# Two of four x tiles transposed by the DMA instead of PE at the start of the key stage, with their plain load moved to ScalarE's queue

## The chip, the cores and the metric

The kernel runs on one core of one Trainium2 chip. The metric is the device time of one execution in microseconds.

Engines: PE (TensorE, matmul), DVE (VectorE), ACT (ScalarE), POOL (GpSimd) and SP (SyncE). SP and ACT also issue DMA transfers. I call the transfers issued by one of them its ring.

## The reference, cut to what matters

```python
def _A_ref(x, wqkv, wo):          # linear attention, 32 heads of 16
    q, k, v = split(x @ wqkv)
    phi = lambda t: where(t > 0, t + 1, exp(t)) + 1e-6
    pq, pk = phi(q), phi(k)
    kv = einsum("bhsd,bhse->bhde", pk, v); z = pk.sum over s
    o = (pq @ kv) / (pq . z + 1e-6)
    return o @ wo
def _B_ref(x, w1, b1, w2, b2):    # token mixer: layernorm, w1 over tokens, gelu, w2
    ...
g = sigmoid((x * gate_w).sum(-1))
return g * _A_ref(...) + (1 - g) * _B_ref(...)
```

x is 2048 x 512 in bf16, in 16 tiles of 128 rows. The key stage computes `x @ Wk`. That needs every x tile transposed (`xT`) as the stationary operand, and Wk in four blocks of 128 rows, called Wk rows 0 to 3 here.

## The kernel before

The parts that the change touches (cuts marked):

```python
    def load_xT(t0, n):           # DMA transpose straight from HBM, always on SP
        nc.sync.dma_start(out=xT[:, :, t0*P:(t0+n)*P], in_=X[t0*P:(t0+n)*P, :], transpose=True)

    load_x(nc.sync, 0, 1)
    load_x(nc.scalar, 1, 1)
    load_wk(nc.sync, 0)
    load_x(nc.scalar, 2, 1)
    load_x(nc.sync, 3, 1)
    for k, q in ((1, nc.scalar), (2, nc.sync), (3, nc.scalar)):
        load_wk(q, k)
    load_xT(4, 2)
    load_xT(6, 2)
    load_x(nc.sync, 4, 4)
    ...                           # tiles 8-15, Wq, w1, Wv, Wo, all on SP
    nc.scalar.activation(out=act_warm[:], in_=ones_f[:], func=ACT.Exp)   # brings the table load
    warm_up(6)                    # six dummy matmuls on constants
    ...
    HEADS = 4
    transpose_tile(0, False)      # four PE transposes into PSUM, evacuated by DVE
    transpose_tile(1, True)       # ... evacuated by ACT
    transpose_tile(2, False)
    for k in range(2):
        for t in range(HEADS - 1):
            k_part(t, (k,))       # key matmul of tile t with Wk row k
    transpose_tile(HEADS - 1, True)
    for t in range(HEADS):
        k_part(t, range(2 if t < HEADS - 1 else 0, ND))
        k_phi(t)
    LAG = 4
    for t in range(HEADS, NT):
        k_part(t, range(ND)); k_phi(t)
        g_tile(t - LAG)           # gacc matmuls: x^T times phi(k)
        ...
```

The order of instructions on each engine is as written. In this kernel's trace the loads from SP and ACT share eight completion semaphores in turn, so the ninth and later ones wait until the earlier load of the same semaphore has landed.

## Time and profile before

| | before |
|---|---|
| median, us | 165.53 (165.50 to 165.75, 4 runs) |
| span of the profile, us | 163.4 |
| PE busy | 158.7 us, 97% |
| first gacc matmul | 9.93 us |
| last matmul of the kernel | 160.37 us |

From the page (first line: the span; then busy time; then 40 slices of 4.1 us, in tenths of the slice, and the DMA's GB/s):

```profile
span 163.4 us, 2099 instructions
PE 158.7 (97%) x787; PEld 73.3 (45%) x801; DVE 88.3 (54%) x202; ACT 58.7 (36%) x90; POOL 18.3 (11%) x37
PE   7999999999999999999999999999999999999993
PEclk9999999999999999999999999999999999999999
GB/s 152 235 237 213 280 308 328 349 349 348 326 130 0 0 0 247 202 4 0 286 299 101 181 320 279 323 121 88 36 32 32 32 32 32 45 52 35 32 32 32
```

PE is full from the second slice to the last. So only the start can change the time, and a shift there reaches the end. The chain of waits of the first 12 us (start, length, what) says how the start goes:

```profile
0.81 2.98 DMA xs<-in_A_x_dram
3.84 1.05 PE pt L195 x8
4.91 0.61 ACT xT L199
5.56 1.29 PE kacc L108 x5
6.85 0.22 PE pt L195 x4
7.08 3.02 PE kacc L108 x14
10.10 0.86 PE gacc L108 x4
```

The x tiles land, PE transposes tiles 0 and 1 (`pt`), and ACT copies tile 1. From 5.56 us there is only PE. ACT was ready in time, as its timeline shows (start, length, instruction; in brackets the idle time before it and what ended it):

```profile
2.67 1.28 ACT L189 ACT_TABLE_LOAD   x1 [2.67 <-issue]
3.96 0.20 ACT L189 ACTIVATE act_warm<-ones_f 128x1 f32<-128x1 f32 x1
4.91 0.60 ACT L199 ACTIVATE xT<-pt 128x512 bf16<-128x512 bf16 x1 [0.74 <-PE pt L195]
```

### The profile page before, as it was taken

The numbers are of one execution on the slowest core, as the hardware profiler recorded it, in microseconds if no ns is written. First come the engines' busy times: TensorE is split into PE (matmuls) and PEld (weight loads), VectorE is DVE, ScalarE is ACT, GpSimd is POOL, SyncE is SP. The second block draws the span as 40 slices with busy tenths as digits, with TensorE's granted clock in tenths as the row PEclk, the third lists the DMA queues.
The fourth block names the chain that finished last, engine by engine and source line by source line (L and its number), as shares of the span: only waits on it lengthen the run. The fifth ranks groups of instructions, "written<-read, shape, count | busy, mean of one in ns | idle before, by whom it ended". The sixth has DMA issues, their size and how long they took to land.

```text
span 163.4 us, 2099 instructions
## 1 busy us (share of the span) xinstructions
PE 158.7 (97%) x787; PEld 73.3 (45%) x801; DVE 88.3 (54%) x202; ACT 58.7 (36%) x90; POOL 18.3 (11%) x37
## 2 busy tenths in 40 slices
PE   7999999999999999999999999999999999999993
PEld 2544444444444444444444444444444444444452
DVE  1599999957999999029995301156221111111112
ACT  3463386648676483111222213111112222111110
POOL 5000711200100000001055500050000000000000
PEclk9999999999999999999999999999999999999999
DMA  5999999999950007600893599932100000111001
GB/s 152 235 237 213 280 308 328 349 349 348 326 130 0 0 0 247 202 4 0 286 299 101 181 320 279 323 121 88 36 32 32 32 32 32 45 52 35 32 32 32
DMA packets 30057, 25.05 MB, mean 153 GB/s; under 512 B 7968, under 2 KB 29472, under 8 KB 30048
## 3 DMA queue, kind: packets, MB, share of 16 engines
q1 hardware_dynamic: 28032, 22.02, 45.5%
q0 software_dynamic: 1440, 2.38, 5.5%
q10 hardware_dynamic: 576, 0.52, 1.1%
q8 instruction: 6, 0.10, 0.3%
q14 instruction: 3, 0.02, 0.0%
HBM read 21.11 MB, written 2.23 MB: 143 GB/s over the span
## 4 chain that ended last, share of the span: by engine, by line
PE 95%; DMA 2%; issue 1%; ACT 0%; DVE 0%
PE uacc L108 30%; PE yps L108 29%; PE aps L108 9%; PE gacc L108 8%; PE qacc L108 8%; PE kacc L108 8%; DMA xs<-in_A_x_dram 2%; PE pt L195 1%; PE denps L108 1%; PE wps L108 1%; PE kvps L108 0%; ACT xT L199 0%; DVE ot L481 0%; PE zps L108 0%; PE pt L324 0%
## 5 line engine op out<-in xcount | busy, mean ns | idle before, releaser
L108 PE MATMUL uacc<-hs,w1c 128*128 128x512 bf16 x219 | 51.8, 379 | 0.4
L108 PE MATMUL yps<-uT,w2c 128*128 128x512 bf16 (+2 forms) x234 | 50.6, 366 | 0.2
L481 DVE SCALAR_TENSOR_TENSOR ot<-yps,c,a_sc 128x512 bf16<-128x512 f32 (+2 forms) x17 | 12.2, 720 | 46.0 <-PE yps L108 42.7
L108 PEld LDWEIGHTS <-w2c 128*128 128x128 bf16 x238 | 22.8, 98 | 25.9
L108 PEld LDWEIGHTS <-w1c 128*128 128x128 bf16 x224 | 21.7, 98 | 26.3 <-issue 0.4
L468 ACT ACTIVATE a_sc<-aps,c,gg 128x512 f32<-128x512 f32 x16 | 12.4, 778 | 46.7 <-PE aps L108 43.0
L318 ACT ACTIVATE uT<-uacc,bcol 128x512 bf16<-128x512 f32 x14 | 9.3, 687 | 28.3 <-PE uacc L108 28.3
L108 PE MATMUL aps<-W2sb,pqT 128*128 128x512 bf16 x63 | 16.4, 379 | 0.1
L108 PE MATMUL qacc<-xT,wq_sb 128*128 128x512 bf16 x63 | 16.2, 379 | 0.0
L108 PE MATMUL kacc<-wk_sb,xT 128*128 128x512 bf16 x63 | 16.0, 380 | 0.1
L108 PE MATMUL gacc<-pk,xs 128*128 128x512 bf16 x62 | 15.5, 379 | 0.1
L245 ACT ACTIVATE hs<-xs,nmr,rstd 128x512 bf16<-128x512 bf16 x16 | 12.8, 805 | 1.9 <-DVE nmr L239 1.9
L205 ACT ACTIVATE e<-qacc 128x512 bf16<-128x512 f32 x16 | 9.6, 597 | 9.2 <-PE qacc L108 8.3
L419 POOL DMA_DIRECT2D rex<-rd_dram x16 | 9.4, 602 | 23.0 <-DVE pqT L421 17.5
L205 ACT ACTIVATE e<-kacc 128x512 bf16<-128x512 f32 x16 | 9.3, 595 | 6.9 <-PE kacc L108 5.6
L209 DVE SCALAR_TENSOR_TENSOR pk<-kacc,e 128x512 bf16<-128x512 f32 x16 | 11.1, 692 | 0.6
L209 DVE SCALAR_TENSOR_TENSOR pqT<-qacc,e 128x512 bf16<-128x512 f32 x16 | 11.1, 692 | 0.6
L229 DVE BATCH_NORM_STATS2 stats<-xs 128x6 f32<-128x512 bf16 x16 | 10.9, 682 | 0.0
L206 DVE TENSOR_SCALAR e<-e 128x512 bf16<-128x512 bf16 x32 | 9.0, 282 | 3.1 <-ACT e L205 3.1
L406 DVE CUSTOM_DVE_ANT_0 junk<-xs,gw_b 128x512 bf16<-128x512 bf16 x16 | 9.9, 684 | 0.0
L270 DVE TENSOR_TENSOR zacc<-zacc,pk 128x512 f32<-128x512 f32 x14 | 9.6, 686 | 0.2
L108 PEld LDWEIGHTS <-pqT 128*128 128x128 bf16 x64 | 6.3, 98 | 7.6
(65 smaller groups left out, 69.6 us busy)
## 6 DMA issues: line engine op xcount, KB each, us to landing
w2c<-in_B_w_dram SPq DMA_DIRECT2D x8, 896.0 KB, 6.6
w1c<-in_B_w_dram SPq DMA_DIRECT2D x2, 2048.0 KB, 15.7
w1c<-in_B_w_dram SPq DMA_DIRECT2D x3, 1024.0 KB, 12.9
rex<-rd_dram POOLq DMA_DIRECT2D x16, 128.0 KB, 3.2
out_dram<-ot SPq DMA_DIRECT2D x15, 128.0 KB, 1.7
xs<-in_A_x_dram SPq DMA_DIRECT2D x3, 512.0 KB, 5.1
wq_sb<-in_A_wqkv_dram SPq DMA_DIRECT2D x1, 512.0 KB, 7.1
wv_sb<-in_A_wqkv_dram SPq DMA_DIRECT2D x1, 512.0 KB, 11.4
```

The lines of the kernel that those rows point to most:

```text
L108: nc.tensor.matmul(o, lhsT=lhsT, rhs=rhs, start=start, stop=stop, **kw)
L205: nc.scalar.activation(out=e[:], in_=acc[:], func=ACT.Exp)
L206: nc.vector.tensor_scalar(out=e[:], in0=e[:], scalar1=1.0, scalar2=PHI_EPS, op0=ALU.min, op1=ALU.add)
L209: nc.vector.scalar_tensor_tensor(out=dst, in0=acc[:], scalar=0.0, in1=e[:], op0=ALU.max, op1=ALU.add)
L229: nc.vector.bn_stats(out=stats[:], in_=xs[:, t, :])
L245: nc.scalar.activation(out=hs[:, t, :], in_=xs[:, t, :], func=ACT.Identity, scale=rstd[:, t : t + 1], bias=nmr[:, t : t + 1],)
L270: nc.vector.tensor_tensor(out=zacc[:], in0=first, in1=pk[:, t, :], op=ALU.add)
L318: nc.scalar.activation(out=uT[:, j, :], in_=acc[:], func=ACT.Gelu_apprx_tanh, bias=bcol[:, j : j + 1])
L406: nc.vector.tensor_tensor_reduce(out=junk[:], in0=xs[:, t, :], in1=gw_b[:], scale=1.0, scalar=0.0, op0=ALU.mult, op1=ALU.add, accum_out=gp ...
L419: nc.gpsimd.dma_start(out=rex[:], in_=src.unsqueeze(1).to_broadcast([8, HEAD, SC]))
L468: nc.scalar.activation(out=a_sc[:], in_=aps[:], func=ACT.Identity, scale=gg[:, t : t + 1], bias=c2[:, t : t + 1],)
L481: nc.vector.scalar_tensor_tensor(out=ot[:, :W], in0=yps[:, :W], scalar=c1[:, t : t + 1], in1=a_sc[:, cs], op0=ALU.mult, op1=ALU.add,)
```

## The change

The intent: let the DMA transpose tiles 2 and 3, so that PE opens with two tiles instead of four. Eight PE transposes and two evacuations go. Tiles 2-3 still have to be loaded plain (for `gacc` and the layernorm); that is not urgent, and goes last on ACT's ring. The four Wk rows are also dealt out anew: row 1 alone stays on SP, rows 0, 2 and 3 go on ACT. Wk row 3 is the fourth load on ACT's ring in both kernels.

```diff
     load_x(nc.sync, 0, 1)
     load_x(nc.scalar, 1, 1)
-    load_wk(nc.sync, 0)
-    load_x(nc.scalar, 2, 1)
-    load_x(nc.sync, 3, 1)
-    for k, q in ((1, nc.scalar), (2, nc.sync), (3, nc.scalar)):
-        load_wk(q, k)
+    load_wk(nc.sync, 1)
+    load_wk(nc.scalar, 0)
+    load_xT(2, 2)
+    for k in (2, 3):
+        load_wk(nc.scalar, k)
     load_xT(4, 2)
+    load_x(nc.scalar, 2, 2)
     load_xT(6, 2)
@@
-    HEADS = 4
+    HEADS = 2
     transpose_tile(0, False)
     transpose_tile(1, True)
-    transpose_tile(2, False)
     ln_step(0)
     for k in range(2):
-        for t in range(HEADS - 1):
+        for t in range(HEADS):
             k_part(t, (k,))
-    transpose_tile(HEADS - 1, True)
     ln_step(1)
     for t in range(HEADS):
-        k_part(t, range(2 if t < HEADS - 1 else 0, ND))
+        k_part(t, range(2, ND))
         k_phi(t)
@@
-        g_tile(t - LAG)
+        if t >= LAG:
+            g_tile(t - LAG)
```

## The prediction

> **What bounds the kernel now.** TensorE. The page gives PE 158.7 of 163.4 us busy; the chain that ended last is 95% PE. In the timeline, from 7.1 us on matmul follows matmul every 0.216 us, and the list of waits has no DMA wait of PE after the start. So only the start (about 10 us) can change the time, and whatever it gains or loses there is passed on whole.
>
> **The start before.** x tile 1 lands at 3.60 us, tile 0 at 3.79; PE transposes tiles 0, 1, 2 from 3.84, 0.107 us each (slow clock). VectorE copies tile 0 (4.48-4.90), first key matmul at 5.09. ScalarE copies tile 1 at 4.91-5.51, so the second key matmul starts at 5.56. From there the chain of waits is PE alone: 19 key matmuls and the four transposes of tile 3 (0.056 us each, 0.22 in all), then the first gacc matmul at 9.93. ScalarE was ready: its four loads were issued by 2.64, its table load ran 2.67-3.95, its warm-up activation to 4.16.
>
> **Removed.** Eight PE transposes and two evacuations (0.42 DVE, 0.60 ACT). Those of tile 2 lie in the shadow of the tile 0 and 1 copies; only those of tile 3, 0.22 us, are on the chain. Total with smoother order: about 0.25 us.
>
> **Added, moved.** (a) A 256-row DMA transpose as third transfer on SP, issued at about 1.75. Its like took 1.34 us to issue and 3.7-4.1 us to landing, so I estimate 5.8-6.9; tile 2 is needed at 7.1 or later. The skill (DMA: Bandwidth & Descriptors, "Issuing engines are not separate DMA queues") says all issuers share the same 16 DMA engines; some delay of the Wk loads (landing 4.4-6.5 before) is likely, little of it exposed. The next SP transfers come 0.6 us earlier; nothing waits for them.
> (b) The plain load of tiles 2-3 is the fifth issue on ACT's queue. Read instruction by instruction, it waits for the semaphore of an earlier load, that of x tile 1, which lands at 3.60. ScalarE's stream is in order, so table load, warm-up activation and the copy of tile 1 stand behind it. Issue 3.6-4.1 (0.5, as its likes), table load 1.28 -> 5.4, warm-up 0.2 -> 5.63, copy 0.60 -> 6.24. The second key matmul then starts at about 6.3 instead of 5.56: +0.74 us, on the chain, since PE's order is fixed. The skill (ScalarE: Activation LUTs, "What ACT_TABLE_LOAD costs") has 1283 ns for the load; this trace has 1283 ns twice.
>
> **Sum.** +0.74 - 0.25 = +0.5 us; first gacc at about 10.4. Everything later shifts rigidly.
>
> **Predicted: 166.05 us, 165.3 to 166.9 (8 in 10).** Faster by over 2%: 0.01; within 2%: 0.97; slower: 0.02.
>
> **What would show it.** ACT: a gap before the table load to about 4.1, table load to 5.4, copy of tile 1 at 5.6-6.2. PE: idle about 0.8 us before the second key matmul, then at least 19 key matmuls without a stop; first gacc near 10.4; no wait for xT tiles 2-3. Right in (a) if transposed tiles land before 7.5. From first gacc to the end the same length as before.
>
> **What would make it wrong.** If the ACT load does not hold the table load back, the gain of 0.25 us stands (165.3). If the DMA transpose slows Wk or lands after 7.8, PE stalls more (+0.3 to 1). PE's clock became fast at about 5.4 us; with PE idler around 4.8-6.3 it may rise later, and each key matmul in slow state costs 0.2 us more (up to +1.2).

## The result, and the profile after

The changed kernel takes 168.50 us (168.07 to 168.54, 4 runs), against 165.53 before. The ratio is 1.0171, with a 95% interval of 1.0152 to 1.0190. (Ratios are the mean of one kernel's runs over the mean of the other's of the same rounds, so not quite the ratio of the medians. Executions over 1.5% slower than the fastest of the same kernel are left out of the means.) The direction was as predicted, but the loss was 2.97 us instead of 0.5.

The same lines of the page:

```profile
span 166.5 us, 2081 instructions
PE 159.6 (96%) x779; PEld 73.0 (44%) x793; DVE 88.1 (53%) x201; ACT 58.5 (35%) x89; POOL 18.4 (11%) x37
PE   7499999999999999999999999999999999999992
PEclk9969999999999999999999999999999999999999
GB/s 140 164 202 281 267 352 314 354 348 348 332 154 0 0 0 96 345 0 4 159 351 96 162 306 284 348 123 132 31 35 31 31 31 31 31 50 48 31 31 32
```

Nearly all the difference is in the first three slices. PE is half idle in the second, its clock is down in the third, and the DMA moves 164 and 202 GB/s where it moved 235 and 237, though more is asked of it. The first gacc matmul comes at 12.88 us, 2.95 later; the last matmul of the kernel comes at 163.32, also 2.95 later. From the first gacc to the last matmul nothing has changed. (After the last matmul this trace has 3.22 us to the end of the span, and the one before 3.07.)

ACT's timeline:

```profile
3.60 0.44 ACTq L124 DMA_DIRECT2D xs<-in_A_x_dram  x1
4.08 1.28 ACT L190 ACT_TABLE_LOAD   x1 [4.08 <-DMA xs<-in_A_x_dram]
5.37 0.20 ACT L190 ACTIVATE act_warm<-ones_f 128x1 f32<-128x1 f32 x1
5.48 0.58 ACT L200 ACTIVATE xT<-pt 128x512 bf16<-128x512 bf16 x1
```

This is the hold that was predicted. The late load waits for x tile 1 (landed at 3.58), and the table load stands behind it. PE's timeline shows what was not predicted:

```profile
3.45 1.01 PE L196 MATMUL pt<-ident,xs 128*128 128x128 bf16 x8
4.58 0.39 PE L108 MATMUL kacc<-wk_sb,xT 128*128 128x512 bf16 x1
6.11 1.04 PE L108 MATMUL kacc<-wk_sb,xT 128*128 128x512 bf16 x4 [1.15 <-ACT xT L200]
8.23 4.82 PE L108 MATMUL kacc<-wk_sb,xT 128*128 128x512 bf16 x15 [1.08 <-DMA wk_sb<-in_A_wqkv_dram]
12.88 0.81 PE L108 MATMUL gacc<-pk,xs 128*128 128x512 bf16 x3
```

After the hold there is a second wait, for Wk. Then 15 matmuls take 4.82 us, where 14 took 3.02 (before, in the chain). The stretches that the clock record itself is divided into show why (per engine busy time and instructions, then the granted clock, DMA share and GB/s):

```profile
core 0: us, PE busy (x) PEld busy (x) DVE busy (x) ACT busy (x) POOL busy (x), PEclk, DMA share, GB/s
4.31:7.72 3.41, 1.58 (x7) 0.50 (x6) 1.75 (x5) 1.74 (x3) 0.00 (x0) 1.00 1.26 169
7.72:11.14 3.42, 2.91 (x7) 0.98 (x7) 1.59 (x4) 1.19 (x2) 0.00 (x0) 0.50 1.24 151
```

In the window from 4.31 to 7.72 PE was busy for only 1.58 us, and for the next 3.42 us its clock was 0.50. Seven key matmuls started about 0.42 us apart instead of 0.216.

The transfers, by tile and issue. In the kernel before, the last Wk row (asked together with row 2 of SP, which took 4.3 us; row 3 took 4.0) and the transpose of tiles 4-5:

```profile
L127 ACTq DMA_DIRECT2D wk_sb<-in_A_wqkv_dram x1: 453/453/453, 2.2 to 2.2; - x1
DMA to landing us min/median/max: 4.0/4.2/4.3
```

```profile
L130 SPq DMA_TRANSPOSE xT<-in_A_x_dram x1: 1337/1337/1337, 3.6 to 3.6; - x1
DMA to landing us min/median/max: 4.1/4.1/4.1
```

In the changed kernel, the last Wk row (issued by ACT at 2.2), then the transposes of tiles 2-3 and of tiles 4-5:

```profile
L127 ACTq DMA_DIRECT2D wk_sb<-in_A_wqkv_dram x1: 454/454/454, 2.2 to 2.2; - x1
DMA to landing us min/median/max: 6.0/6.0/6.0
```

```profile
L130 SPq DMA_TRANSPOSE xT<-in_A_x_dram x1: 1333/1333/1333, 1.7 to 1.7; - x1
DMA to landing us min/median/max: 7.1/7.1/7.1
```

```profile
L130 SPq DMA_TRANSPOSE xT<-in_A_x_dram x1: 2813/2813/2813, 3.1 to 3.1; - x1
DMA to landing us min/median/max: 8.6/8.6/8.6
```

| landed at, us | before | after |
|---|---|---|
| Wk row 3 | 6.21 | 8.19 |
| transpose of tiles 2-3 | (on PE) | 8.81 |
| transpose of tiles 4-5 | 7.67 (issued 3.62) | 11.67 (issued 3.11) |

On PE's own clock of events the 2.95 us add up. The second key matmul comes 0.55 us later (6.11 against 5.56), the wait for Wk row 3 is 1.24 (8.23 minus 6.77 minus 0.216), and the slow clock is 1.42 (seven starts in 2.93 us instead of 1.51). The removed transposes of tile 3 and small rests give back 0.26. But this is a list of what stood on PE's path one after another. It does not say what the time would be without one of them, since the transpose of tiles 4-5 landed at 11.67, only 0.35 ahead of its first use at 12.02. The experiments had to tell that.

### The profile page after: what moved, and what is told of

The parts are those of the page before. It is cut to its first block, busy times and chain, and to the rows that moved or that the text cites. A ratio compares the mean times of both kernels' runs of the same rounds, so it can differ in the third digit from the quotient of the medians.

```text
span 166.5 us, 2081 instructions
## 1 busy us (share of the span) xinstructions
PE 159.6 (96%) x779; PEld 73.0 (44%) x793; DVE 88.1 (53%) x201; ACT 58.5 (35%) x89; POOL 18.4 (11%) x37
## 4 chain that ended last, share of the span: by engine, by line
PE 93%; DMA 4%; ACTq 1%; issue 1%; DVE 0%
PE yps L108 29%; PE uacc L108 29%; PE kacc L108 8%; PE qacc L108 8%; PE aps L108 8%; PE gacc L108 8%; DMA wk_sb<-in_A_wqkv_dram 4%; PE denps L108 1%; ACTq L127 1%; PE wps L108 1%; PE kvps L108 0%; ACTq L124 0%; DVE ot L481 0%; PE zps L108 0%; PE pt L324 0%
## 5 line engine op out<-in xcount | busy, mean ns | idle before, releaser
L108 PE MATMUL kacc<-wk_sb,xT 128*128 128x512 bf16 x63 | 17.3, 406 | 2.3 <-ACT xT L200 1.1
L206 ACT ACTIVATE e<-kacc 128x512 bf16<-128x512 f32 x16 | 9.5, 595 | 11.7 <-PE kacc L108 10.4
L108 PEld LDWEIGHTS <-xT 128*128 128x128 bf16 x64 | 6.5, 103 | 11.3 <-issue 3.0
```

What stands on the lines that cost most here:

```text
L108: nc.tensor.matmul(o, lhsT=lhsT, rhs=rhs, start=start, stop=stop, **kw)
L206: nc.scalar.activation(out=e[:], in_=acc[:], func=ACT.Exp)
```

## The experiments

The theory after this reading was the three terms above. Rival A held that the ACT hold is the cause of everything. Rival B held that the slow clock is a matter of the window's phase or of the eight missing transposes, not of PE's idling. Rival C came up after the first runs: late landings go by the bytes in flight, whatever their kind. All kernels gave correct results. Each was timed beside the kernel before on the same chip, and "before" below is that of its own rounds. One execution of each run has a trace; the last column gives its first gacc and, in brackets, its time. In runs 2, 3, 7 and 9 it is the slowest execution of the run.

| run | us, median (range) | before, us | first gacc in the trace (its time) |
|---|---|---|---|
| late load after ACT's table load | 168.53 (167.39 to 169.59) | 165.63 | 11.68 (167.39) |
| Wk row 3 ahead of the transposes | 166.32 (166.19 to 167.97) | 165.63 | 11.97 (167.97) |
| both | 165.70 (165.04 to 167.06) | 165.63 | 11.73 (167.06) |
| filler matmuls | 167.79 (167.23 to 168.06) | 165.63 | 12.29 (167.97) |
| rings apart | 165.65 (165.33 to 166.12) | 165.59 | 9.53 (165.36) |
| plain loads in the transposes' place | 170.34 (167.87 to 171.49) | 165.59 | 12.87 (169.26) |
| before, 256 KB more on ACT | 166.62 (166.58 to 167.50) | 165.59 | 11.53 (167.50) |
| before, 256 KB more on SP | 166.19 (165.92 to 166.28) | 165.59 | 9.83 (166.21) |
| rings apart, loads merged | 165.40 (164.89 to 165.83) | 165.61 | 10.22 (165.83) |
| late load on SP | 166.55 (165.75 to 168.26) | 165.61 | 11.04 (166.54) |
| rings apart and ACT held | 165.76 to 167.62 (5 runs) and one of 598.72 | 165.61 | (no usable trace) |
| the same again | 165.82 and 165.99 | 165.64 and 165.70, and one of 285.17 at a clock of 0.563 | 10.45 (165.82) |

### 1. The late load after ACT's table load

```diff
-    load_x(nc.scalar, 2, 2)
     ...
     nc.scalar.activation(out=act_warm[:], in_=ones_f[:], func=ACT.Exp)
+    load_x(nc.scalar, 2, 2)
```

> The changed kernel, with the plain load of tiles 2-3 issued by ScalarE after its table load and warm-up activation instead of before. Theory (three terms: ScalarE held about 0.55 us; the last Wk row landing at 8.19 us instead of 6.2-6.5; slow PE clock for seven key matmuls after the two idle stretches): the table load goes back to about 2.7 us and the second key matmul to about 5.1 us, but PE then waits longer for the last Wk row, which still lands near 8.2; the clock still falls; time unchanged, 168.0 to 168.6. Rival A (the ScalarE hold is the cause of all of it): 165.3 to 165.6.

The median was 168.53, in two groups: 167.39 and 167.72 with a mean clock of 1.0, 169.35 and 169.59 with 0.99. PE's timeline of the traced one (167.39):

```profile
4.58 1.43 PE L108 MATMUL kacc<-wk_sb,xT 128*128 128x512 bf16 x5 [0.30 <-DVE xT L202]
8.10 2.53 PE L108 MATMUL kacc<-wk_sb,xT 128*128 128x512 bf16 x11 [2.09 <-DMA wk_sb<-in_A_wqkv_dram]
10.80 1.04 PE L108 MATMUL kacc<-wk_sb,xT 128*128 128x512 bf16 x4 [0.17 <-DMA xT<-in_A_x_dram]
```

The hold is gone (second key matmul at 4.97), and PE simply waits for Wk row 3 until 8.10. One wait of 2.09 us stands where the changed kernel had two, 1.15 and 1.08. Rival A falls: in the changed kernel the predicted hold was mostly hidden behind the DMA. The two groups lie about 1.9 us apart; the slower one has no trace, so that this is the clock alone is not shown. The traced execution had a 2 us idle stretch and no fall, so the same kernel falls into the slow clock in some executions and not in others.

### 2. Wk row 3 ahead of the first transpose, ACT still held

```diff
     load_wk(nc.scalar, 0)
+    load_wk(nc.sync, 3)
+    load_wk(nc.scalar, 2)
+    (a load of 128 x 8 elements on ACT, so that the late load still waits)
     load_xT(2, 2)
-    for k in (2, 3):
-        load_wk(nc.scalar, k)
```

> The changed kernel, with the last Wk row issued on SP ahead of the first DMA transpose; a tiny load on ACT's queue keeps ScalarE's wait as it is. Theory: the last Wk row lands by about 6.5, PE's second stall goes, and with it the slow clock; the hold of ScalarE stays (second key matmul at about 6.1). What can still cost is the transpose of tiles 2-3, which landed at 8.81 in the changed kernel and is wanted at about 7.7: 166.0 to 167.0. Rival A: unchanged, 168.5. Rival B (the last Wk row is late because it is fourth on its ring, and the slow clock is the window's phase): the stall goes, the slow clock stays, 167.2 or more.

166.32: four executions at 166.19 to 166.37, two at 167.59 and 167.97. All Wk had landed by 5.31 and the second stall went, as the theory had it. The transpose of tiles 2-3 landed at 6.13, in time. The traced execution is the slowest one. There the clock rose only at 9.62 (window 6.21 to 9.62 slow), which cost it about 1.7 us (nine starts in 3.64 us instead of 1.94). That PE's idling delayed the rise fits, but one trace does not show it.

### 3. Both edits

```diff
     load_wk(nc.scalar, 0)
-    load_xT(2, 2)
-    for k in (2, 3):
-        load_wk(nc.scalar, k)
+    load_wk(nc.sync, 3)
+    load_wk(nc.scalar, 2)
+    load_xT(2, 2)
     load_xT(4, 2)
-    load_x(nc.scalar, 2, 2)
     ...
     nc.scalar.activation(out=act_warm[:], in_=ones_f[:], func=ACT.Exp)
+    load_x(nc.scalar, 2, 2)
```

> Both edits together (without the tiny load). Theory: second key matmul at about 5.1, all Wk by 6.5, tiles 0-1 done near 7; then PE waits for the transpose of tiles 2-3 if that lands after 7. Time 165.2 if it lands by 7, 166.2 to 167 if it lands at 8 to 8.8. Rival A: 165.3 to 165.6 whatever lands when.

167.06, 165.05, 166.34 and 165.04. In the traced execution (167.06) the transpose of tiles 2-3 landed at 9.08 and the late load at 9.01, side by side on the two rings, and PE waited 2.13 us for it:

```profile
9.12 2.76 PE L108 MATMUL kacc<-wk_sb,xT 128*128 128x512 bf16 x12 [2.13 <-DMA xT<-in_A_x_dram]
```

The expectation held in its conditional form. The executions of 165.04 and 165.05 have no trace; they lie below all seven of the kernel before in these rounds (165.37 to 165.90), with the late load still on the other ring. So the two need not hurt each other in every execution. Why the same transpose lands at 6.1 in one run and at 9.1 in another was open. That led to the new theory: a transpose from one ring beside plain loads from the other makes both slow.

### 4. Filler matmuls in the second idle stretch

```diff
     ln_step(1)
+    warm_up(5)
     for t in range(HEADS):
         k_part(t, range(2, ND))
```

> The changed kernel with five more dummy matmuls on constants placed in PE's second idle stretch, between the key matmuls of Wk rows 1 and 2. Theory (the idle stretches made the clock fall): the key matmuls after 8.2 us run at 0.216 us each instead of 0.427, so more work makes it faster: 167.0 to 167.4. Rival B (the slow clock is the phase of a window, or the eight fewer PE transposes, not the idling): unchanged or slower, 168.3 to 168.6.

```profile
6.67 1.25 PE L108 MATMUL wps<-const-bfloat16-1.0 128*128 128x512 bf16 x5
7.76 0.38 PE L108 MATMUL kacc<-wk_sb,xT 128*128 128x512 bf16 x1
8.30 2.54 PE L108 MATMUL kacc<-wk_sb,xT 128*128 128x512 bf16 x11 [0.16 <-DMA wk_sb<-in_A_wqkv_dram]
11.41 1.04 PE L108 MATMUL kacc<-wk_sb,xT 128*128 128x512 bf16 x4 [0.57 <-DMA xT<-in_A_x_dram]
```

Five more matmuls made it faster: 167.79 against 168.50. All four executions had a clock of 1.0; of the changed kernel's four, three had 0.99. That is few, but the other runs agree: but for the execution of 285.17, mean clocks of 0.99 or less appear only in kernels whose traces show PE waiting about a microsecond or more (the changed kernel, runs 1, 6, 10 and 11, the last by the trace of run 12), and in none of the twelve executions of runs 5 and 9, which lack the same eight transposes (0.998 or more). So the missing transposes are not it. The window's phase may still decide in which executions the clock falls, since run 1 fell in two of four. The gain was 0.7 us, below the expected 1.1 to 1.5. With the clock fast, PE meets the next wait, the transpose of tiles 4-5 that lands at 11.37. In the changed kernel it landed at 11.67 and was first used at 12.02, so with a fast clock and the same landings only about 0.3 of the 1.42 us could have come back, and the one execution of the changed kernel with a clock of 1.0 took 168.07, 0.4 less than the others. So more than half of what the slow clock took on PE's path was in the shadow of a late transfer.

### 5. The rings kept apart

```diff
     load_wk(nc.scalar, 0)
-    load_xT(2, 2)
-    for k in (2, 3):
-        load_wk(nc.scalar, k)
+    load_wk(nc.sync, 3)
+    load_wk(nc.scalar, 2)
+    load_xT(2, 2)
     load_xT(4, 2)
-    load_x(nc.scalar, 2, 2)
     load_xT(6, 2)
+    load_x(nc.sync, 2, 2)
```

> The changed kernel with no plain load left on ACT's ring beside a transpose: ACT carries only x tile 1 and Wk rows 0 and 2, SP the rest, Wk row 3 ahead of the transposes and the plain load of tiles 2-3 behind them. New theory (from the packets of the first runs: transposes and plain loads that run at once from two rings both crawl): all Wk lands by 6.0, the transpose of tiles 2-3 between 6 and 7, that of 4-5 by 8, and this in every execution; no hold of ScalarE; time 165.0 to 165.2 with a spread below 0.5. Rival C (the landings of transposes are early or late by chance, or go by bytes): a spread of 1 to 2 us as in the run with both edits.

The landings were as expected: Wk by 5.37, tiles 2-3 at 6.57, tiles 4-5 at 8.00. PE does not stop:

```profile
4.94 4.76 PE L108 MATMUL kacc<-wk_sb,xT 128*128 128x512 bf16 x20 [0.20 <-DVE xT L202]
9.53 0.81 PE L108 MATMUL gacc<-pk,xs 128*128 128x512 bf16 x3
```

The first gacc at 9.53 and the last matmul at 159.97 are both 0.40 us earlier than before. The spread is 0.8 us, as for the kernel before in these rounds, and not below 0.5 as expected. Yet the time is 165.65 against 165.59 (ratio 1.0007, 0.9989 to 1.0025). In the traced execution the stretch from the last matmul to the end of the span takes 3.54 us instead of 3.07, although the last output had landed 2.10 us after the last matmul in both. The expected time was missed for a reason outside the argument (see runs 7 and 8).

### 6. Plain loads in the transposes' place

```diff
     load_wk(nc.scalar, 0)
-    load_xT(2, 2)
+    (plain load of 256 KB on SP into a buffer written later)
     for k in (2, 3):
         load_wk(nc.scalar, k)
-    load_xT(4, 2)
+    (another of 256 KB)
     load_x(nc.scalar, 2, 2)
+    load_xT(2, 2)
+    load_xT(4, 2)
```

> The changed kernel with the first two DMA transposes on SP replaced, in their places, by plain loads of the same 256 KB each (into a buffer that is overwritten later; the result stays right), and the transposes issued behind them. It is about the landing of the last Wk row, not the time. New theory (transposes beside plain loads are what is slow): the last Wk row lands by 6.7. Rival C (it is late because 512 KB more share the engines): at 7.5 to 8.2 as in the changed kernel. The time is worse than 168 either way, as the transposes come later.

Wk row 3 landed at 7.87, not by 6.7. This went against the new theory. For this transfer, 512 KB of plain loads ahead on the other ring do nearly the same as the transposes, so Rival C is right for Wk row 3. The engines did move far more in that time, though: 315 GB/s from 6 to 7 us, where the changed kernel moved 190.

### 7 and 8. The kernel before with 256 KB more, on ACT's ring or on SP's

```diff
+    nc.scalar.dma_start(out=hs[:, 14:16, :], in_=x_view[:, 14:16, :])   # 7: after ACT's warm-up activation
+    nc.sync.dma_start(out=hs[:, 14:16, :], in_=x_view[:, 14:16, :])     # 8: between load_xT(4, 2) and load_xT(6, 2)
```

(`hs` is written much later, so the result stays right.)

> The kernel before with one plain load of 256 KB more (into a buffer that is overwritten later), issued on ACT after its warm-up activation, so that it runs beside the transposes of tiles 4-7 on SP. New theory: those transposes, which landed at 7.7 and 8.7 us, land 1.5 to 3 us later, and PE waits for tiles 4-5, wanted at 9.1: 165.6 to 167. Rival C (bytes): 256 KB at the 240 to 340 GB/s of this stretch is 0.8 to 1.1 us, landings by 8.7 and 9.7, time unchanged.

> The same load of 256 KB, but on SP's ring, between the transposes of tiles 4-5 and 6-7, so that nothing runs beside them from another ring. New theory: the transpose of tiles 4-5 lands as before (7.7), that of 6-7 about 0.8 to 1.1 us later than 8.7; time unchanged, 165.4 to 165.8. Rival C: as the run with the load on ACT, or worse.

The stretch from 4 to 11 us, of the run with the load on ACT and then of the one with the load on SP (last columns: clock, DMA share, GB/s):

```profile
4.00:11.00 7.00, 5.41 (x32) 2.53 (x30) 4.34 (x11) 3.56 (x7) 0.00 (x0) 1.00 1.11 196
```

```profile
4.00:11.00 7.00, 6.79 (x42) 3.73 (x41) 5.17 (x13) 4.03 (x8) 0.00 (x0) 1.00 1.11 258
```

| landed at, us | before | 256 KB more on ACT | 256 KB more on SP |
|---|---|---|---|
| transpose of tiles 4-5 | 7.67 | 10.61 | 7.68 |
| transpose of tiles 6-7 | 8.71 | 11.25 | 9.85 |
| the added load | - | 10.46 | 8.74 |

These are the same bytes in the same kernel. Behind one another on one ring they are done at 9.85; side by side from two rings they are done at 11.25, and the transpose of tiles 4-5 comes 2.9 us later. That is what the new theory expected and more than Rival C allows (256 KB are 1.1 us at 240 GB/s). Two reservations apply. The traced execution with the load on ACT is its slowest (167.50, the others 166.6), and that execution was slow before the added load, issued at 4.33, could matter (230 GB/s from 4 to 5 us, 326 in run 8). The run on SP missed its expected time (166.19 instead of 165.4 to 165.8), though its first gacc is at 9.83. The loss is again after the last matmul, 4.03 us instead of 3.07.

The windows view answers a rival that these runs leave, that any two rings hurt each other. By the sizes of the packets in the traces, both rings carry plain loads from 3 to 5 us of the kernel before, and move 346 and 336 GB/s in these two microseconds. Transposes with nothing beside them moved 220 and 192 (kernel before, 6 to 8 us). Transposes beside plain loads moved 86 to 203, 163 in the mean (changed kernel, 4 to 11 us): in the mean less than either alone.

The records of SP explain part of the longer ends. There SP waits for the completion semaphores one after another in a fixed order, about 0.06 us each. In the kernel before, the last two output stores signal the last of them. With one or two transfers more (runs 2, 6, 7 and 8) the last store signals one of the first, and six or seven more waits, about 0.5 us, follow its landing instead of preceding it. Another 0.4 us between two later steps of SP appears in runs 5, 6 and 8, the three with 45 transfers issued on SP (44 before); why is not shown.

### 9. Rings apart, two loads merged

```diff
-    load_x(nc.sync, 2, 2)
-    load_x(nc.sync, 4, 4)
+    load_x(nc.sync, 2, 6)
```

> The run with the rings kept apart, with the two plain loads of tiles 2-3 and 4-7 on SP merged into one of tiles 2-7. In that run PE's last matmul came 0.40 us earlier than in the kernel before, but the end sequence after it took 3.54 us instead of 3.07, with one SP instruction more. Theory: with that instruction gone the end sequence is 3.0 to 3.2 us and the gain comes through: 165.1 to 165.3 where the kernel before has 165.5 to 165.6. Rival: the loss at the end has another cause, end sequence 3.5 us and 165.6 again.

The stretch after the last matmul was 3.16 us, as expected. The time was 165.40 against 165.61, a ratio of 0.9988 with an interval of 0.9969 to 1.0008, so no gain is shown (165.1 to 165.3 had been expected). In the traced execution the transpose of tiles 2-3 landed at 7.57, a microsecond later than in run 5, and PE waited 0.45 us for it. No version here is shown to be faster than the kernel before.

### 10. Only the late load moved to SP

```diff
-    load_x(nc.scalar, 2, 2)
     load_xT(6, 2)
+    load_x(nc.sync, 2, 2)
```

> The changed kernel with only the plain load of tiles 2-3 moved from ACT to SP, behind the transposes; Wk rows 2 and 3 stay on ACT beside the transposes. Theory: ScalarE is not held (second key matmul at about 5.1-5.4); Wk row 3 still lands at 7.5 to 8.2, because the transposes ahead on SP share the engines with it; but once it has landed nothing runs beside the transposes, so those of tiles 2-3 and 4-5 land by about 7.5 and 9 instead of 8.8 and 11.7: first gacc at 11 or before, and 166.2 to 167.3 where the clock stays fast, about 0.5 of it the longer end sequence (one SP instruction more). Rival (the late load plays no part): tiles 4-5 at 11 or later, 167.8 to 168.5.

166.54, 166.56 and 165.75, and one of 168.26 with a clock of 0.99. Wk row 3 still landed at 7.77. The transpose of tiles 4-5, issued at the same 3.1 us as in the changed kernel, took 5.5 us instead of 8.6:

```profile
L130 SPq DMA_TRANSPOSE xT<-in_A_x_dram x1: 2307/2307/2307, 3.1 to 3.1; - x1
DMA to landing us min/median/max: 5.5/5.5/5.5
```

```profile
7.81 3.40 PE L108 MATMUL kacc<-wk_sb,xT 128*128 128x512 bf16 x15 [1.29 <-DMA wk_sb<-in_A_wqkv_dram]
11.04 1.03 PE L108 MATMUL gacc<-pk,xs 128*128 128x512 bf16 x4
```

This one line of the change carries about two of the three microseconds (168.50 to 166.55). Part of that is the clock: at a clock of 1.0 it is 168.07 (one execution) against 165.75 to 166.56, and the one execution at 0.99 (168.26) is hardly faster than the changed kernel's at 0.99. Run 1, which frees ACT but leaves the load beside the transposes, had its transpose of tiles 4-5 at 10.76 and its fast-clock executions at 167.4 to 167.7. So more of it is the traffic than the hold. My guess that the end sequence would be 0.5 longer here was wrong: it took 3.06, and the trace has 44 transfers on SP, as many as the kernel before.

### 11 and 12. Rings apart, ACT held on purpose

This is the kernel of run 9 with one line more.

```diff
+    nc.scalar.dma_start(out=held[:], in_=xs[:, 1, 0:8])   # waits for x tile 1; ahead of the table load
```

> The run with merged loads, plus one tiny copy on ACT's queue (eight columns of x tile 1) that has to wait for x tile 1 and so holds the table load back as the late load does in the changed kernel, without its traffic. This is the hold term of the prediction alone (+0.74 us): second key matmul at 6.0 to 6.3 instead of 5.4, the rest unchanged, 0.5 to 0.9 us slower than the run without it: 165.8 to 166.0. If ScalarE had slack there, the same time.

> The held run once more, unchanged, because its profiled execution fell into a state in which every matmul took about four times as long (598.7 us), so that the hold has no usable trace. Expected as before: table load from about 4.2 to 5.5 us, copy of tile 1 from about 5.7, second key matmul at 6.0 to 6.4; first gacc at 10.1 to 10.4 if all transposes land in time and the clock is fast; 165.8 to 166.0, or 167 to 168 if the clock rises late.

The first attempt is of little use. Its traced execution took 598.72 us with matmuls about four times as slow from start to end, which no view explains. Of the other five, three took 165.8 to 165.9 and two 167.3 and 167.6. The second attempt gave 165.82 and 165.99, with this on PE:

```profile
6.34 4.27 PE L108 MATMUL kacc<-wk_sb,xT 128*128 128x512 bf16 x19 [1.31 <-ACT xT L201]
10.45 0.81 PE L108 MATMUL gacc<-pk,xs 128*128 128x512 bf16 x3
```

The second key matmul at 6.34 and the first gacc at 10.45 are both 0.92 us later than in run 5 (I compare with run 5 because the trace of run 9 has the late transpose), and the first gacc is 0.52 later than before. This is the start that the prediction described: the hold, nineteen key matmuls without a stop, first gacc near 10.4. The time, 165.9 us from two executions, is not clear of that before (ratio 1.0014, 0.9971 to 1.0057).

## Why the prediction was right or wrong

**Right: what bounds the kernel, and that a shift at the start is passed on whole.** The shift of the first gacc and that of the last matmul are both 2.95 us.

**Right: the hold of ACT.** The table load was predicted to end at 5.4 and did at 5.36; the copy of tile 1 was predicted at 5.63 to 6.24 and ran from 5.48 to 6.06; the second key matmul was predicted at about 6.3 and came at 6.11. With nothing else in the way (run 12) the whole sum, +0.74 minus 0.25, came out as +0.52 in the trace: the second key matmul 0.78 later, and 0.26 won back after it.

**Right: the gain of the removed transposes is small.** It was predicted at 0.25; without hold or stalls (run 5) PE was 0.40 ahead.

**Wrong: step (a), in two places.** The step took the landing of a DMA transpose (3.7 to 4.1 us) from the trace of before, where transposes run nearly alone (their packets begin at 5.1 us, and ACT's ring has sent its last by 5.7), and carried it into a stretch where plain loads run beside them. The prediction put tiles 2-3 at 5.8 to 6.9; they landed at 8.81. Of tiles 4-5 it said that nothing waits for them; they landed at 11.67, 4.00 later than before, so that even with a fast clock PE could have come only about 0.3 us earlier. The second place is the sentence that a delay of the Wk loads would be "little of it exposed": Wk row 3 landed 2 us later and 1.24 us of it stood on PE's path. Run 6 shows that this part needs no transposes, only 512 KB on the other ring. The prediction did name slower Wk loads and late transposes as what would make it wrong (+0.3 to 1), but its range left them out.

**Wrong: the late load was costed only as an instruction on ACT.** Step (b) saw what it waits for and what waits behind it, and forgot that its 256 KB run beside the transposes. Run 10 shows that moving it alone takes away about two of the three microseconds, the hold and part of the clock's fall with it.

**Half seen: the clock.** The prediction named it as a risk of up to 1.2 us. The fall came after the stalls that the prediction did not have, and run 4, which fills one of them, did not have it in any of four executions. On PE's path it took 1.42 us, but only 0.4 to 0.7 of that was worth having back, because the transpose of tiles 4-5 was waiting behind it.

So the gain of the change on PE was 0.3 to 0.4 us (runs 12 and 5). The transfers that it put side by side cost several times that.

**Open.** What inside the DMA engines makes a transpose beside plain loads slow is not shown; runs 7 and 8 show only the rates and landings, of one execution each. Nor is it shown why it happens in some executions and not in others (run 3). Some transposes vary by a microsecond from run to run even with the rings apart (6.57 in run 5, 7.57 in run 9).

## What to carry to other kernels

Take the duration of a transfer from the trace only for the company that it had there. When a change puts a DMA transpose beside plain loads of another ring, expect that both may slow down, and put transfers that are not urgent behind the transposes on the same ring. A DMA issue on a compute engine's queue is an instruction in its stream and traffic in the engines, and both have to be costed. Idle stretches of a microsecond on PE can cost twice, once as the wait and once as the clock after it.

## What the Trainium skill lacked or had wrong

- DMA: Bandwidth & Descriptors, "Rules for kernel authors", says that a transpose next to ordinary DMAs needs nothing. All results here were correct, so that agrees. The page has no word on what the two cost each other in time: the same bytes in the stretch from 4 to 11 us moved at 258 GB/s on one ring and at 196 with the plain load on the other (runs 8 and 7), and a 256-row transpose took 7.1 to 8.6 us instead of 4.1.
- The same page, "Issuing engines are not separate DMA queues", says that issuing from several engines only saves issue time. For plain loads no run here contradicts it. With transposes on one of the rings it was worse than neutral in the traces of runs 7 and 8: the same bytes were done at 11.25 us from two rings and at 9.85 from one. (Wk row 3 landed at 8.19 on ACT's ring beside two transposes, and at 5.03 to 5.83 on SP ahead of them in runs 2, 3, 5 and 9; that is its place in the order as much as its ring.)
- TensorE: Matmul & The Clock Gate, "Why this matters for your kernels", asks for no PE-idle gaps above about 3 us. The changed kernel's longest idle stretch was 1.15 us, and the clock fell to 0.50 after a window of 3.41 us in which PE was busy for 1.58. The window length on that page (3413 ns, free-running) agrees with the records (3.41 us). Its remark that the phase varies fits: the rise of the clock in the traces that record it lies between 3.91 (run 12) and 5.56 us (run 10), and at 9.62 in run 2.
- The same page, "Part 4: PE-mode transpose", says that the fast clock does not engage for transpose-mode. In run 12 the clock rose at 3.91 us, in the middle of the transposes, and their starts went from 0.107 to 0.056 us apart. So transposes do run at the fast clock; whether they count as busy for its rise is not shown, since dummy matmuls came before them.
- ScalarE: Activation LUTs, "What ACT_TABLE_LOAD costs", gives 1283 ns plus about 1380 ns of drain. The trace has the 1283 ns; the warm-up activation started 0.01 us after the load, so no drain showed here.
- No page that I used has this: the stretch from the last matmul to the end of the span goes with the number of transfers on the two rings. It took 3.06 to 3.23 us in eight of the thirteen traces, and 3.53 to 4.03 in those of runs 2, 5, 6, 7 and 8, which is more than the change could gain.
